# Cosine attention and a multiplicative FFN in one kernel: another order of copies and products in the start-up, and the features of the second batch one by one among the weight-product blocks

## The chip, the cores and the metric

The kernel runs on one core of one Trainium2 chip. The time is the device time of one execution in microseconds (us). Five engines work side by side, each through its own instructions in order: TensorE (PE in the profile, with PEld for its weight loads), VectorE (DVE), ScalarE (ACT), GpSimd (POOL) and SyncE (SP). Here POOL issues all loads, and SP all stores.

## The reference

For 8 batches, 8 heads, 576 positions and 64 elements per head, q and k are made into features of 128 elements (the positive part times a cosine, and times a sine, of the position). Attention without softmax follows, and its output x, 4608 tokens of 512, goes through a feed-forward network (FFN) that multiplies two products:

```python
q_p = phi(q, cos_w, sin_w)
k_p = phi(k, cos_w, sin_w)
kv = np.einsum('bhsf,bhsd->bhfd', k_p, v)
z = np.sum(k_p, axis=2)
num = np.einsum('bhsf,bhfd->bhsd', q_p, kv)
den = np.einsum('bhsf,bhf->bhs', q_p, z)[..., None] + 1e-06
...
a = x @ w1
b = x @ w2
h = a * b @ w3
return (h @ w_out).astype(np.float32)
```

The kernel forms w34 = w3 @ w_out once, so that the last two products become one.

## The kernel before, in words

All of it is one stream that is written out by hand: the order of the calls in the code is the order on every engine.

A batch has 576 positions: five chunks, four of 128 rows and one of 64. `prep_k`, `prep_q` and `prep_v` make one chunk's features: the cosine half of `kp` or `qp` on DVE (L182), the sine half on ACT (L184), and a copy of v into `va` (L196; on DVE for batches 0 and 1, on POOL later). `kv_chunk` multiplies a chunk's `kp` and `va` into a PSUM tile `pnum` over all heads (L212); after the last chunk one half of it is copied to `kvs` by ACT (L217) and the other by DVE (L218). `q_tr` turns a chunk of `qp` over (8 transposes on PE into a PSUM tile `pst`, L226), and DVE copies the result to `qpT` (L227). `num` multiplies `qpT` by `kvs` (L237), and DVE divides by the denominator in three instructions (L241, L242, L244), which gives `xblk`. `x_tr` turns `xblk` over (L263), and ACT copies it into `xT` (L264).

The FFN goes over nine tiles t of 512 tokens. `ffn_groups(t)` is a generator of 24 steps: for each of eight blocks jc of the inner dimension, four products with `w1b` (L303, evicted by ACT as `asb`, L306) and four with `w2b` (L310, multiplied by DVE into `abT`, L312), then for four output blocks eight products with `w34b` (L317), evicted by ACT (L322) and stored. At each step the loop at the end of the kernel puts other work, from a list `slots`, behind the products. During tile t the attention of batch t+1 and the features of later batches run in these slots.

The start-up is batch 0 by itself: features of k and q, `q_tr` and `prep_v` in turns, `kv_chunk`, then `num` and `x_tr` in turns. Its chunks 0 to 3 fill tile 0. Chunk 4 goes in slots 1 and 3. 32 products of a tile of zeros at the very start (`idle_mms`, L120) give PE something to do while the first loads come.

In slot 15 of tile 0 stands the forming of w34: for each of eight row blocks jp, `w3_tr` transposes a block of w3 (L154), DVE copies five eighths of it and ACT three eighths (L156, L157), and `w34_mm` does eight products with `woutb` (L164), which ACT copies into `w34b` (L166). Behind block jp = 1 come all ten k features of batch 1, behind 2 all q features, behind 3 all v copies, and behind 4 to 7 the first attention units of batch 1. `pst` has two buffers, `w3T` two, `ffnps` four.

POOL issues the loads in the order k, q, v of batch 0, `w1b` and `w2b` in three pieces each, `woutb`, then the eight blocks `w3b` mixed with k, q and v of batch 1, then batch 2.

Of the kernel before, what the change touches and what calls it, by code (L numbers as in the profile page):

```python
# [16 lines left out]
P = 128  # L17
H, S, D = 8, 576, 64
F = 2 * D
NCH = 5  # L20
# [31 lines left out]
def kernel(  # L52
# [28 lines left out]
    ps_first = first.enter_context(tc.tile_pool(name="ps_first", bufs=2, space=bass.MemoryType.PSUM))  # L81
# [33 lines left out]

    def idle_mms(n):

        w = ps_first.tile([P, 2, 512], FP32, name="pfirst")
        for _ in range(n):
            nc.tensor.matmul(w[:, 0, :], lhsT=zeros[:, 0:128], rhs=zeros[:], start=True, stop=True)  # L120
# [30 lines left out]
    def w3_tr(jp):  # L151
# [4 lines left out]
        nc.vector.tensor_copy(out=w3T[:, 0:5, :], in_=pst[:, 0:5, :])  # L156
        nc.scalar.copy(out=w3T[:, 5:8, :], in_=pst[:, 5:8, :])  # L157
        w3Ts[jp] = w3T

    def w34_mm(jp):  # L160
        acc = ps_ffn.tile([P, 512], FP32, name="ffnps")
        w3T = w3Ts.pop(jp)
        for lc in range(8):
            nc.tensor.matmul(acc[:, :], lhsT=w3T[:, lc, :], rhs=woutb[:, lc, :],  # L164
                             start=(lc == 0), stop=(lc == 7))
        nc.scalar.copy(out=w34b[:, jp, :], in_=acc[:, :])  # L166
# [54 lines left out]
    def q_tr(b, c):  # L221
# [5 lines left out]
        nc.vector.tensor_copy(out=att_of(b)["qpT"][:, :, ds(128 * c, R)], in_=pst[:, :, 0:R])  # L227

    def num(b, c):
        R = ROWS[c]  # L230
        qpT, kvs = att[b]["qpT"], att[b]["kvs"]
        if b == 0 and c < 4:
# [64 lines left out]
    def ffn_groups(t):  # L297
        x = xT[t]
        abT = fsb.tile([P, 8, 512], BF16, name="abT", bufs=2)
        for jc in range(8):  # L300
            aT = ps_ffn.tile([P, 512], FP32, name="ffnps")
            for kc in range(4):
                nc.tensor.matmul(aT[:, :], lhsT=w1b[:, kc, ts(jc, 128)], rhs=x[:, kc, :],  # L303
                                 start=(kc == 0), stop=(kc == 3))
# [4 lines left out]
            for kc in range(4):  # L309
                nc.tensor.matmul(bT[:, :], lhsT=w2b[:, kc, ts(jc, 128)], rhs=x[:, kc, :],  # L310
                                 start=(kc == 0), stop=(kc == 3))
# [16 lines left out]
    def prep_units(b):  # L328
        return [(lambda f=f, c=c: f(b, c)) for f in (prep_k, prep_v, prep_q) for c in range(NCH)]
# [23 lines left out]
    for t in range(NT):  # L353
        slots = [[] for _ in range(24)]
        if t == 0:
            slots[1].append(lambda: num(0, 4))
            slots[3].append(lambda: x_tr(0, 4))
            slots[14].append(lambda: w3_tr(0))
            w = slots[15]
# [62 lines left out]
```

## Time and profile before

| | |
|---|---|
| median of 3 runs | 287.17 us |
| these runs | 286.15, 287.17, 352.44 us |
| the profiled execution | 288.88 us |
| its span, first to last instruction | 287.1 us |
| PE busy | 270.8 us, 94% |
| PE's weight loads | 143.8 us, 50% |
| DVE / ACT / POOL busy | 149.8 / 144.0 / 61.0 us |
| granted TensorE clock, mean | 0.982 |

Of the profiled time 1.8 us lie outside the span. PE is busy 94% of the span, so what can be gained stands where PE is idle, or busy at a lower clock: the places must be looked up by stage. Busy time is not work: a product at half the clock is busy twice as long.

### The profile page before, as it was taken

Reading aid. Unit: us, or ns where it says so; the run is one execution under the profiler, and the core shown is the slowest. Engines: PE = TensorE matmul, PEld = TensorE weight load, DVE = VectorE, ACT = ScalarE, POOL = GpSimd, SP = SyncE. Lnnn points to the kernel's source line nnn. Section 1 sums busy time; section 2 is a strip of 40 time slices with the busy share of each in tenths; the row PEclk is TensorE's granted clock in tenths of the full one; section 3 lists DMA queues with packets and bytes.
Section 4 is the critical chain, followed back from the end, with each engine's and each line's share of the span. In section 5 each row is a group of like instructions: output and inputs, shape, how many; then the busy total and the mean of one; then the engine's idle time right before and its main releaser. Section 6 shows DMA issues by size and latency. Waiting matters only on the chain.

```text
span 287.1 us, 5398 instructions
## 1 busy us (share of the span) xinstructions
PE 270.8 (94%) x2144; PEld 143.8 (50%) x2144; DVE 149.8 (52%) x356; ACT 144.0 (50%) x254; POOL 61.0 (21%) x101
## 2 busy tenths in 40 slices
PE   8668999789999999999999999999999999999993
PEld 3353455455555555555555555555555555444441
DVE  4672457126468747773686467447634752321420
ACT  2813337722697386268537644863572235324331
POOL 8631443710035323305110810000000000000000
PEclk9995999889999999999999999999999999999999
DMA  7999999991459597937493910330041005006005
GB/s 97 196 202 208 204 203 202 199 198 33 106 85 188 71 211 119 135 66 116 79 163 70 130 35 3 75 73 2 0 110 39 0 12 133 8 0 146 0 22 128
DMA packets 36490, 29.20 MB, mean 102 GB/s; under 512 B 2160, under 2 KB 30832, under 8 KB 36464
## 3 DMA queue, kind: packets, MB, share of 16 engines
q0 software_dynamic: 30704, 19.40, 48.1%
q1 hardware_dynamic: 5760, 9.44, 13.4%
q8 instruction: 17, 0.28, 0.4%
q14 instruction: 9, 0.07, 0.1%
HBM read 38.80 MB, written 9.44 MB: 168 GB/s over the span
## 4 chain that ended last, share of the span: by engine, by line
PE 73%; DMA 15%; ACT 5%; POOL 3%; DVE 2%; issue 1%; POOLq 0%; ACTq 0%
PE ffnps L317 22%; PE ffnps L310 18%; PE ffnps L303 17%; DMA ks<-in_k_dram 6%; PE pst L226 5%; DMA w2b<-in_moe_w_dram 4%; PE pnum L237 3%; DMA w3b<-in_moe_w_dram 3%; PE pnum L212 3%; PE ffnps L164 3%; PE pst L263 3%; ACT kp L184 2%; DMA vs<-in_v_dram 2%; ACT qp L184 1%; DVE kp L182 1%
## 5 line engine op out<-in xcount | busy, mean ns | idle before, releaser
L312 DVE TENSOR_TENSOR abT<-asb,ffnps 128x512 bf16<-128x512 bf16 x72 | 49.3, 685 | 77.6 <-PE ffnps L310 70.9
L306 ACT CAST asb<-ffnps 128x512 bf16<-128x512 f32 x72 | 42.1, 585 | 76.9 <-PE ffnps L303 74.8
L303 PE MATMUL ffnps<-xT,w1b 128*128 128x512 bf16 x288 | 74.7, 382 | 0.7 <-ACT xT L264 0.7
L310 PE MATMUL ffnps<-xT,w2b 128*128 128x512 bf16 x288 | 74.9, 383 | 0.0
L317 PE MATMUL ffnps<-w34b,abT 128*128 128x512 bf16 x288 | 70.9, 379 | 0.0
L303 PEld LDWEIGHTS <-w1b 128*128 128x128 bf16 x288 | 26.2, 98 | 26.1 <-issue 1.4
L310 PEld LDWEIGHTS <-w2b 128*128 128x128 bf16 x288 | 25.2, 98 | 24.4 <-issue 1.1
L317 PEld LDWEIGHTS <-abT 128*128 128x128 bf16 x288 | 25.6, 98 | 23.5
L322 ACT COPY osb<-ffnps 128x512 f32<-128x512 f32 x36 | 21.1, 586 | 24.9 <-PE ffnps L317 21.1
L227 DVE COPY qpT<-pst 128x1024 bf16<-128x1024 bf16 (+1 forms) x40 | 25.2, 630 | 10.8 <-PE pst L226 10.8
L184 ACT ACTIVATE kp<-ks,sinv 128x512 bf16<-128x512 bf16 (+1 forms) x40 | 26.9, 717 | 5.0 <-DMA ks<-in_k_dram 5.0
L264 ACT COPY xT<-pst 128x512 bf16<-128x512 bf16 (+1 forms) x40 | 21.7, 543 | 14.9 <-PE pst L263 14.1
L184 ACT ACTIVATE qp<-qs,sinv 128x512 bf16<-128x512 bf16 (+1 forms) x40 | 27.2, 719 | 0.5 <-DMA qs<-in_q_dram 0.5
L226 PE MATMUL pst<-identb,qp 128*128 128x128 bf16 (+1 forms) x320 | 22.7, 213 | 3.9 <-ACT qp L184 2.4
L226 PEld LDWEIGHTS <-qp 128*128 128x128 bf16 (+1 forms) x320 | 19.0, 97 | 14.0 <-ACT qp L184 3.7
L244 DVE TENSOR_TENSOR xblk<-pnum,den 128x512 bf16<-128x512 f32 (+1 forms) x36 | 24.8, 689 | 1.2
L237 PEld LDWEIGHTS <-qpT 128*128 128x128 bf16 (+1 forms) x320 | 15.0, 102 | 12.6 <-issue 4.1
L164 PE MATMUL ffnps<-woutb,w3T 128*128 128x512 bf16 x64 | 16.8, 405 | 2.0 <-ACT w3T L157 2.0
L212 PEld LDWEIGHTS <-kp 128*128 128x128 bf16 (+1 forms) x320 | 14.0, 97 | 9.0 <-issue 3.1
L196 POOL COPY va<-vs 128x512 bf16<-128x512 bf16 (+1 forms) x30 | 17.4, 636 | 2.4 <-PE pnum L212 2.4
L182 DVE TENSOR_SCALAR kp<-ks,cosv 128x512 bf16<-128x512 bf16 (+1 forms) x40 | 17.1, 459 | 0.6 <-DMA ks<-in_k_dram 0.6
L263 PEld LDWEIGHTS <-xblk 128*128 128x128 bf16 (+1 forms) x160 | 11.0, 99 | 12.1 <-DVE xblk L244 3.1
(51 smaller groups left out, 176.2 us busy)
## 6 DMA issues: line engine op xcount, KB each, us to landing
out_dram<-osb SPq DMA_DIRECT2D x72, 128.0 KB, 2.4
ks<-in_k_dram POOLq DMA_DIRECT2D x8, 320.0 KB, 5.1
qs<-in_q_dram POOLq DMA_DIRECT2D x8, 320.0 KB, 6.4
vs<-in_v_dram POOLq DMA_DIRECT2D x8, 320.0 KB, 7.2
ks<-in_k_dram POOLq DMA_DIRECT2D x8, 256.0 KB, 6.1
qs<-in_q_dram POOLq DMA_DIRECT2D x8, 256.0 KB, 7.0
vs<-in_v_dram POOLq DMA_DIRECT2D x8, 256.0 KB, 8.4
w3b<-in_moe_w_dram POOLq DMA_DIRECT2D x8, 256.0 KB, 15.6
```

What stands on the lines that cost most here:

```text
L164: nc.tensor.matmul(acc[:, :], lhsT=w3T[:, lc, :], rhs=woutb[:, lc, :], start=(lc == 0), stop=(lc == 7))
L184: nc.scalar.activation(out=dst[:R, c, :, D:F], in_=src[:R, :, c, :], func=ACTF.Relu, scale=sinv[:R, c:c + 1], bias=0.0)
L212: nc.tensor.matmul(kvt[:, h // 4, ds((h % 4) * 65, 65)], lhsT=kp[:R, c, h, :], rhs=va[:R, c, h, 0:D + 1], start=(c == 0 and h % 4 == 0), s ...
L226: nc.tensor.transpose(pst[:, h, 0:R], qp[:R, c, h, :], identb[:R, :R])
L227: nc.vector.tensor_copy(out=att_of(b)["qpT"][:, :, ds(128 * c, R)], in_=pst[:, :, 0:R])
L237: nc.tensor.matmul(nt[:R, h // 4, ds((h % 4) * 65, 65)], lhsT=qpT[:, h, ds(128 * c, R)], rhs=kvs[:, h, :], start=True, stop=True)
L244: nc.vector.tensor_tensor(out=xblk[:R], in0=n4[:, :, :, 0:D], in1=den[:R].unsqueeze(3).to_broadcast([R, 2, 4, D]), op=ALU.mult)
L303: nc.tensor.matmul(aT[:, :], lhsT=w1b[:, kc, ts(jc, 128)], rhs=x[:, kc, :], start=(kc == 0), stop=(kc == 3))
L306: nc.scalar.copy(out=asb[:], in_=aT[:, :])
L310: nc.tensor.matmul(bT[:, :], lhsT=w2b[:, kc, ts(jc, 128)], rhs=x[:, kc, :], start=(kc == 0), stop=(kc == 3))
L312: nc.vector.tensor_mul(out=abT[:, jc, :], in0=asb[:], in1=bT[:, :])
L317: nc.tensor.matmul(ops[:, :], lhsT=abT[:, jc, ts(ms, 128)], rhs=w34b[:, jc, :], start=(jc == 0), stop=(jc == 7))
```

## The change

Three pieces, all in tile 0 or ahead of it; from tile 1 on the instructions and their order are the same on every engine.

1. The order in the start-up. `q_tr` of chunks 0 and 1 goes first, then the five v copies in a row, then `q_tr` of chunks 2 and 3, whose copies to `qpT` are now ACT's, then `kv_chunk`, and `q_tr` of chunk 4 only behind it. `num` of chunks 1 and 3 uses the buffer `pnum`, chunks 0 and 2 share one `pfirst`. Eight products of zeros into a tile that nobody reads (`unread`) stand at five places among this work.
2. The first FFN products of tile 0. For jc = 0 and 1, all four products (w1 and w2) are done on tokens 0 to 255 first, and then on tokens 256 to 511; `x_tr` of chunk 3 stands between. Chunk 4's `num` and `x_tr` move from slots 1 and 3 to 4 and 6.
3. The w34 blocks. DVE alone copies `w3T`. Each block's eight products are two parts of four, which gives 16 gaps. The 15 feature units of batch 1 are spread one or two at a time over gaps 4 to 12, in the order k, q, v, and the first ten attention units over gaps 10 to 15.

```diff
-    ps_first = first.enter_context(tc.tile_pool(name="ps_first", bufs=2, space=bass.MemoryType.PSUM))
+    ps_first = first.enter_context(tc.tile_pool(name="ps_first", bufs=1, space=bass.MemoryType.PSUM))
...
+    unread = ps_first.tile([P, 512], FP32, name="unread")
...
-        nc.vector.tensor_copy(out=w3T[:, 0:5, :], in_=pst[:, 0:5, :])
-        nc.scalar.copy(out=w3T[:, 5:8, :], in_=pst[:, 5:8, :])
+        nc.vector.tensor_copy(out=w3T[:], in_=pst[:])
...
+        if t == 0:
+            acc = [ps_ffn.tile([P, 512], FP32, name="ffnps") for _ in range(4)]
+            for half in range(2):
+                for i in range(4):
+                    products(acc[i], (w1b, w2b)[i % 2], i // 2, ts(half, 256))
+                    if i % 2 == 1:
+                        if half:
+                            to_abT(i // 2, acc[i - 1], acc[i])
+                        yield
...
-    for c in range(NCH):
-        q_tr(0, c)
-        prep_v(0, c)
-    for c in range(NCH):
-        kv_chunk(0, c)
-    for c in range(4):
-        num(0, c)
-        if c >= 1:
-            x_tr(0, c - 1)
-    x_tr(0, 3)
+    q_tr(0, 0)
+    q_tr(0, 1)
+    idle_mms(1)
+    for c in range(NCH):
+        prep_v(0, c)
+    copy2 = q_tr(0, 2, evac=False)
+    copy2[1]()
+    copy3 = q_tr(0, 3, evac=False)
+    for c in range(NCH):
+        kv_chunk(0, c)
+    copy3[1]()
+    q_tr(0, 4)
+    idle_mms(2)
+    num(0, 0)
+    num(0, 1)
+    idle_mms(2)
+    num(0, 2)
+    x_tr(0, 0)
+    idle_mms(1)
+    num(0, 3)
+    x_tr(0, 1)
+    idle_mms(2)
+    x_tr(0, 2)
...
-            slots[1].append(lambda: num(0, 4))
-            slots[3].append(lambda: x_tr(0, 4))
+            slots[0].append(lambda: x_tr(0, 3))
+            slots[4].append(lambda: num(0, 4))
+            slots[6].append(lambda: x_tr(0, 4))
...
-            extra = {
-                1: [(lambda c=c: prep_k(1, c)) for c in range(NCH)],
-                2: [(lambda c=c: prep_q(1, c)) for c in range(NCH)],
-                3: [(lambda c=c: prep_v(1, c)) for c in range(NCH)],
-                4: att1[0:3],
...
+            between = [[] for _ in range(16)]
+            spread(prep_units(1, (prep_k, prep_q, prep_v)), 4, 12, between)
+            spread(att1[:10], 10, 15, between)
             for jp in range(8):
-                if jp < 7:
-                    w.append(lambda jp=jp: w3_tr(jp + 1))
-                w.append(lambda jp=jp: w34_mm(jp))
-                w += extra.get(jp, [])
+                for part in range(2):
+                    if part == 0 and jp < 7:
+                        slots[15].append(lambda jp=jp: w3_tr(jp + 1))
+                    slots[15].append(lambda jp=jp, part=part: w34_mm(jp, part))
+                    slots[15] += between[2 * jp + part]
```

Here `copy2[1]` and `copy3[1]` are the copies of `q_tr` on ACT; `products` is the loop over the four products, on the columns that it is given.

On DVE, in the start-up from the last q feature to the copy of `kvs`, there stood:

```order
L182 TENSOR_SCALAR qp<-qs,cosv 64x8x64
L227 COPY qpT<-pst 128x8x128
L196 COPY va_162<-vs 128x8x64
L227 COPY qpT<-pst 128x8x128
L196 COPY va_162<-vs 128x8x64
L227 COPY qpT<-pst 128x8x128
L196 COPY va_162<-vs 128x8x64
L227 COPY qpT<-pst 128x8x128
L196 COPY va_162<-vs 128x8x64
L227 COPY qpT<-pst 128x8x64
L196 COPY va_162<-vs 64x8x64
L218 CAST kvs<-pnum 128x260
```

and now stands:

```order
L186 TENSOR_SCALAR qp<-qs,cosv 64x8x64
L232 COPY qpT<-pst 128x8x128 x2
L200 COPY va_162<-vs 128x8x64 x4
L200 COPY va_162<-vs 64x8x64
L222 CAST kvs<-pnum 128x260
L232 COPY qpT<-pst 128x8x64
```

Of the five copies to `qpT`, those of chunks 2 and 3 have left DVE (ACT does them), that of chunk 4 stands behind `kvs`, and nothing stands between the five v copies.

On ACT, in the middle of the w34 blocks, there stood (w3T is its three eighths of the transposed block, w34b the eviction, kp and qp the features of batch 1):

```order
L166 CAST w34b<-ffnps 128x512
L184 ACTIVATE kp<-ks,sinv 128x8x64 x4
L184 ACTIVATE kp<-ks,sinv 64x8x64
L157 COPY w3T<-pst 128x384
L166 CAST w34b<-ffnps 128x512
L184 ACTIVATE qp<-qs,sinv 128x8x64 x4
L184 ACTIVATE qp<-qs,sinv 64x8x64
L157 COPY w3T<-pst 128x384
L166 CAST w34b<-ffnps 128x512
```

and now stands:

```order
L170 CAST w34b<-ffnps 128x512 x2
L188 ACTIVATE kp<-ks,sinv 128x8x64 x2
L170 CAST w34b<-ffnps 128x512
L188 ACTIVATE kp<-ks,sinv 128x8x64 x2
L188 ACTIVATE kp<-ks,sinv 64x8x64
L170 CAST w34b<-ffnps 128x512
L188 ACTIVATE qp<-qs,sinv 128x8x64 x4
L170 CAST w34b<-ffnps 128x512
L188 ACTIVATE qp<-qs,sinv 64x8x64
```

No copy of `w3T`, for which PE's next products would wait, stands behind features on ACT any more. On DVE the same blocks now read:

```order
L157 COPY w3T<-pst 128x1024 x3
L186 TENSOR_SCALAR kp<-ks,cosv 128x8x64 x4
L157 COPY w3T<-pst 128x1024
L186 TENSOR_SCALAR kp<-ks,cosv 64x8x64
L186 TENSOR_SCALAR qp<-qs,cosv 128x8x64 x2
L157 COPY w3T<-pst 128x1024
L186 TENSOR_SCALAR qp<-qs,cosv 128x8x64 x2
L186 TENSOR_SCALAR qp<-qs,cosv 64x8x64
L157 COPY w3T<-pst 128x1024
L200 COPY va_164<-vs 128x8x64 x4
```

The copies of v (`va_164`) are still DVE's, and the copy of `w3T` of block jp = 6 now stands directly ahead of them.

More of the change, by code (lines that the diff above doesn't have):

```diff
@@ L155, in w3_tr, with w34_mm @@
         w3T = wst.tile([P, 8, 128], BF16, name="w3T")
[L156 to L157 removed]
+        nc.vector.tensor_copy(out=w3T[:], in_=pst[:])
         w3Ts[jp] = w3T
[L160 to L163, printed above, removed]
+    w34_acc = {}
+    def w34_mm(jp, part):
+        if part == 0:
+            w34_acc[jp] = ps_ffn.tile([P, 512], FP32, name="ffnps")
+        acc, w3T = w34_acc[jp], w3Ts[jp]
+        for lc in range(4 * part, 4 * part + 4):
             nc.tensor.matmul(acc[:, :], lhsT=w3T[:, lc, :], rhs=woutb[:, lc, :],
                              start=(lc == 0), stop=(lc == 7))
[L166 removed]
+        if part == 1:
+            nc.scalar.copy(out=w34b[:, jp, :], in_=acc[:, :])
     feat = {}
```

41 lines of the change are left out of this document (22 added, 19 removed).

## Prediction

> **What bounds the kernel now.** I read the busy time by stage first, because a share over the whole span hides where PE waits. The columns are the stretch, its length, busy time and instructions of PE, PEld, DVE, ACT and POOL, the granted clock, the DMA share and GB/s.
>
> ```profile
> core 0: us, PE busy (x) PEld busy (x) DVE busy (x) ACT busy (x) POOL busy (x), PEclk, DMA share, GB/s
> 11.70:18.20 6.50, 4.52 (x84) 3.96 (x85) 4.79 (x14) 2.80 (x5) 2.79 (x6) 1.00 1.44 197
> 18.20:21.60 3.40, 1.88 (x39) 1.53 (x37) 2.81 (x10) 0.69 (x2) 1.16 (x2) 0.97 1.25 207
> 21.60:24.40 2.80, 1.47 (x13) 0.88 (x11) 1.41 (x4) 1.66 (x3) 0.69 (x1) 0.50 1.24 207
> 24.40:28.40 4.00, 3.98 (x16) 1.46 (x15) 0.30 (x1) 0.59 (x1) 0.56 (x1) 0.52 1.25 209
> 28.40:41.30 12.90, 12.90 (x72) 6.01 (x70) 5.95 (x11) 4.63 (x9) 5.53 (x9) 1.00 1.25 205
> 41.30:52.30 11.00, 10.54 (x78) 5.66 (x76) 6.94 (x21) 8.34 (x16) 5.08 (x9) 1.00 1.32 201
> 52.30:55.80 3.50, 1.99 (x32) 1.53 (x33) 0.28 (x1) 2.90 (x6) 2.22 (x4) 0.96 1.41 198
> 55.80:59.20 3.40, 3.40 (x14) 1.53 (x12) 0.63 (x2) 0.48 (x1) 2.60 (x5) 0.54 1.39 199
> 59.20:66.80 7.60, 6.54 (x83) 4.33 (x81) 2.64 (x7) 2.46 (x5) 0.00 (x0) 1.00 1.12 157
> 66.80:76.90 10.10, 9.96 (x98) 5.77 (x95) 6.83 (x18) 3.85 (x9) 0.00 (x0) 1.00 0.31 72
> 76.90:287.10 210.20, 205.01 (x1611) 107.69 (x1608) 111.58 (x247) 110.16 (x194) 30.91 (x49) 1.00 0.44 77
> ```
>
> From 66.8 us on PE is full (9.96 of 10.10, then 205 of 210, its tail included), and the instructions there are the same before and after. So whatever lead PE has where the first output product starts (66.8) stays to the end, and the whole question is the first 66.8 us. There PE has two thin stretches, 18.2 to 24.4 and 52.3 to 55.8, and behind each the clock is at one half: from 21.6 to 28.4 and from 55.8 to 59.2. The second half of the first loss is paid while PE is fully busy (24.4 to 28.4). Loads run at some 200 GB/s until about 65 us whatever PE does.
>
> **The start-up.** The timeline gives each step's length and, in brackets, the idle time ahead of it with its releaser.
>
> ```profile
> 12.43 0.67 DVE L227 COPY qpT<-pst 128x1024 bf16<-128x1024 bf16 x1
> ...
> 13.91 0.29 DVE L196 COPY va<-vs 128x512 bf16<-128x512 bf16 x1 [0.80 <-DMA vs<-in_v_dram]
> ...
> 14.85 0.61 PE L226 MATMUL pst<-identb,qp 128*128 128x128 bf16 x8 [1.09 <-DVE qpT L227]
> ...
> 15.97 1.61 PE L212 MATMUL pnum<-va,kp 128*128 128x65 bf16 x40
> ...
> 17.63 0.38 ACT L217 CAST kvs<-pnum 128x260 bf16<-128x260 f32 x1 [3.50 <-PE pnum L212]
> ...
> 18.84 0.17 DVE L241 TENSOR_SCALAR den<-pfirst 128x8 f32<-128x8 f32 x1 [0.38 <-PE pfirst L237]
> ...
> 22.39 0.69 DVE L244 TENSOR_TENSOR xblk<-pfirst,den 128x512 bf16<-128x512 f32 x1
> ...
> 23.78 0.59 ACT L264 COPY xT<-pst 128x512 bf16<-128x512 bf16 x1 [0.45 <-PE pst L263]
> 24.42 1.87 PE L303 MATMUL ffnps<-xT,w1b 128*128 128x512 bf16 x4 [0.67 <-ACT xT L264]
> ...
> 30.46 1.04 PE L303 MATMUL ffnps<-xT,w1b 128*128 128x512 bf16 x4
> 30.57 0.37 ACT L264 COPY xT<-pst 128x256 bf16<-128x256 bf16 x1 [0.50 <-PE pst L263]
> ...
> 32.20 1.03 PE L303 MATMUL ffnps<-xT,w1b 128*128 128x512 bf16 x4
> ...
> 33.93 1.03 PE L303 MATMUL ffnps<-xT,w1b 128*128 128x512 bf16 x4
> ```
>
> DVE bounds it: v copies and `qpT` copies in turns keep the fourth chunk's transposes waiting 1.09 us, and `kv_chunk` starts at 15.97. In the changed order the second `qpT` copy ends about 13.8 (two of 0.67 from 12.43), the v copies start at 13.91 as now, when v is there, and take at most 5 x 0.29 = 1.4 us. The transposes of chunk 3 go from 13.85 to 14.45, and the 40 products behind them start there instead of at 15.97: **1.5 us**. They end at 16.1; chunk 4's transposes and two zero products fit while ACT and DVE make `kvs`. The first denominator comes at 17.4 for 18.84, and four groups of three instructions from 18.84 to 23.08 are 1.06 each, so the four `xblk` end at 18.5, 19.5, 20.6 and 21.6.
>
> ACT's copies of 128x1024 do not occur before. 0.37 us for 256 columns and 0.59 for 512 give 1.03 for 1024; bounds are 0.59 and 1.18 (twice the 512). I take 1.03: chunk 2's runs from 14.1 to 15.2, ahead of `kvs` at 16.1; chunk 3's from 16.5 to 17.5, needed at 19.5. Either bound is hidden; without that 0.9 us of cover, an excess would hold up `kvs` and all behind it one for one.
>
> Now the half tiles. The first FFN products need only chunks 0 and 1 in `xT`: `num` of chunk 3, whose buffer is free when the second `xblk` is done, and `x_tr` of chunk 1 run behind 19.55 (some 0.42 and 0.45), PE is through at 20.45, ACT (0.59) at 21.05, so PE starts at 21.1 instead of 24.42. Two pairs of half products take 0.87 each at full clock (eight whole ones take 32.20 to 33.93 = 1.73), with `x_tr` of chunk 3 between them; its `xT` copy ends at 23.05, just when PE wants the second half, and that ends at 24.85. Splitting 16 products into 32 adds issue cost: I take 0, between 0 and 0.3 us (eight transposes of 128 columns with their loads come in 0.61 us, so a product of 256 should not be bound by its load). In the kernel before, the start of jc = 2 is 30.46, with `num` and `x_tr` of chunk 4 done: twelve short products, some 0.04 us each as the 40 in 1.61, 0.45 together at full clock. The same state is reached at 24.85 + 0.45 = 25.3: a **lead of 5.1 us**. About 2 of it is the clock: 24.42 to 28.4 at half speed.
>
> This takes for granted that the clock stays up. The rows on it:
>
> ```profile
> 2.03 0.15 PEld L120 LDWEIGHTS <-zeros 128*128 128x128 bf16 x1 [0.28 <-issue]
> ...
> 4.46 4.85 PEld L120 LDWEIGHTS <-zeros 128*128 128x128 bf16 x23 [0.15 <-issue]
> ```
>
> Zero products raise the clock: at the start they come every 0.43 us, after 4.46 us every 0.21 (4.85 over 23). PE was 55% busy in the 3.4 us ahead of the first fall and 57% ahead of the second; at 70% (11.7 to 18.2) it did not fall. With the zero products and the denser order my schedule leaves PE idle about 0.65 us between 17.85 and 18.5 and little after that, some 85% busy between 18.2 and 21.6. So I take no fall. The eight zero products cost 8 x 0.216 = 1.7 us of PE, all in waits for DVE by this schedule; if the waits were gone, they would cost up to that.
>
> The Trainium skill, "TensorE: Matmul & The Clock Gate", section "What's actually happening", has the gate fall after an idle window of about 3.4 us, and its windows free-running. By the first half of that, nothing here should have fallen and filling short gaps could save nothing; the trace shows falls behind stretches that were half busy, so I go by the trace. The second half means that where a window cuts can differ between executions; it is why a fall remains a rival.
>
> **The w34 blocks**, from 41.28 on:
>
> ```profile
> 41.28 0.61 PE L154 MATMUL pst<-identb,w3b 128*128 128x128 bf16 x8
> ...
> 43.45 0.61 PE L154 MATMUL pst<-identb,w3b 128*128 128x128 bf16 x8
> ...
> 49.90 0.82 PE L164 MATMUL ffnps<-woutb,w3T 128*128 128x512 bf16 x3 [0.41 <-ACT w3T L157]
> 50.22 3.17 ACT L184 ACTIVATE qp<-qs,sinv 128x512 bf16<-128x512 bf16 x5
> ...
> 53.81 0.82 PE L164 MATMUL ffnps<-woutb,w3T 128*128 128x512 bf16 x3 [1.57 <-ACT w3T L157]
> ...
> 56.17 3.26 PE L164 MATMUL ffnps<-woutb,w3T 128*128 128x512 bf16 x8
> ...
> 60.67 1.89 PE L164 MATMUL ffnps<-woutb,w3T 128*128 128x512 bf16 x8
> ...
> 63.98 0.42 PE L237 MATMUL pnum<-kvs,qpT 128*64 128x65 bf16 x8 [1.06 <-DVE kvs L218]
> ```
>
> PE's last three products of a block wait for ACT's part of `w3T`, which stands behind five features on ACT (3.17 us): 0.41 + 1.57 us idle. DVE's single copy of 128x1024 (0.67, the row of 12.43) takes that away; it lies beside PE's products, since DVE is busy 6.94 of these 11.0 us, and if DVE were full its 0.67 would stand ahead of each block. The third wait, 1.06 us for `kvs`, shrinks because four products stand ahead of `num`; 0.25 us is left by my schedule. The half clock costs 3.26 - 1.89 = 1.4 on the eight products and 0.3 on the transposes ahead of them, 1.7. Taken away: 0.41 + 1.57 + 0.8 + 1.7 = 4.5.
>
> What is late next? Blocks come every 2.17 us (41.28 to 43.45), and loads don't move:
>
> ```profile
> w3b<-in_moe_w_dram POOLq DMA_DIRECT2D x1, 256.0 KB, 10.9
> ...
> 36.42 0.56 POOL L108 DMA_DIRECT2D w3b<-in_moe_w_dram  x1 [0.95 <-DMA ks<-in_k_dram]
> ...
> 46.47 0.68 POOL L95 DMA_DIRECT2D qs<-in_q_dram  x1 [0.46 <-DMA vs<-in_v_dram]
> ```
>
> Block 6 of w3, issued at 36.42, lands 10.9 us later, at 47.3. With the lead, its transposes want to start at 36.2 + 5 x 2.17 = 47.05: a new wait of 0.3 (0 to 0.6). v of batch 1 is there at about 46.4, when the POOL row that waits for it goes on; DVE copies it behind block 6's `w3T`, which ends at about 47.3 + 0.61 + 0.67 = 48.6, so the first copy ends at 48.9; PE, through with the transposes and four products of block 5 at about 48.6, waits some 0.35 for it (0 to 0.6). Behind both waits PE holds the rest of block 5, and ACT its eviction, which nobody wants before 57. Together 0.65. The ACT features lie under PE: from 41.0 ten features of 0.63 (3.17 over 5) and four evictions of 0.59 end near 49.7, and the transposes of the last q chunk want it at about 50.6. Net 4.5 - 0.65 = **3.8 us**.
>
> **Sum**: 5.1 + 3.8 = 8.9 us, so the first output product starts at 57.9 and the profiled execution becomes 288.88 - 8.9 = 280.0. The profiled execution stands 1.7 above the median of 287.17; against that median the result is 278.3. Loads of batch 2 and 3 end before about 67 us as now, and are used in tile 1, from 68 on; stores start earlier, at 61, beside the last loads. I cost that at nothing (0 to 0.5).
>
> **Rivals.**
>
> *The clock falls all the same* in one of the two places (20%). A window of 3.4 busy us at half costs 1.7; two windows at the start, as now, 3.4: 280.0 to 281.7. For it: my zero products may stand where PE is not idle, and window edges vary. Against: no stretch under 70% is left.
>
> *The loads take the lead back* (13%). Were block 6 or v of batch 1 to land later than now, each us costs one, up to the lead of 5.1: 283.4 at worst, 280 to 281 likely. For it: the margin is gone (47.05 against 47.3). Against: the queue waits for the same landings as before, and none of its early waits is on an engine that is late.
>
> *Slower* (2%): half the clock holds from the first FFN product to the last block because every window has a small wait. That is 36.8 us, 10.8 windows of 1.7 = 18.4 lost against 8.9 won, 296.7. It decides from the sixth window on. Against: 28.4 to 41.3 is all busy now, and the same products stand there.
>
> My forecast has 62%, own range 277.2 to 279.8; the last 3% is a gain above mine. A measurement of this kernel tells changes of about 2%, 5.7 us, from none. All of the forecast's chance, half of the clock's, most of the loads' and the 3% are above that: faster 0.85, same 0.13, slower 0.02. The range runs from 276.5 (none of the 0.9 us of waits that I count, and 0.9 for runs that lie 1.0 apart) to 282.0 (a fall at the start, with 0.3 for the split).
>
> **What would show it.** `kv_chunk` from 14.5 instead of 15.97; FFN products of 256 columns from 21.1; clock 1.00 in every stretch from 4.5 on; jc = 2 at about 24.9; the w34 products without a wait for ACT; first output product near 57.9. I am wrong if the clock shows 0.50 behind 21, if PE waits for w3b or v by more than 1 us, or if DVE's copies of w3T hold it up.

## The result, and the profile after

| | before | after |
|---|---|---|
| median | 287.17 us (286.15 to 288.50, 3 runs) | 279.75 us (279.58 to 279.92, 4 runs) |
| the profiled execution | 288.88 us | 279.75 us |
| its span | 287.1 us | 278.0 us |
| granted TensorE clock, mean | 0.982 | 1.0 |
| PE busy | 270.8 us | 265.8 us |

One run more of the kernel before (288.50 us) was made beside those of the changed kernel; the one of 352.44 was disturbed and is left out, so that the median of the others is 287.17 as before. After over before is 0.9738, interval 0.9688 to 0.9788: **faster by 7.4 us**. The forecast was 278.3, 8.9 less than before, its range 276.5 to 282.0: the direction and the range hold, and the size was put 1.45 us too large. Between the two profiled executions the span is 9.1 us shorter, where the sum said 8.9. Both differences are small; why one is short and the other is not is the more useful part of what follows.

The busy time by stage of the changed kernel, with the columns of the prediction's table (stretch, length, busy time and instructions of PE, PEld, DVE, ACT and POOL, clock, DMA share, GB/s):

```profile
11.70:18.20 6.50, 5.88 (x100) 4.52 (x101) 4.66 (x16) 4.79 (x8) 2.95 (x5) 1.00 1.44 193
18.20:21.60 3.40, 2.64 (x36) 1.88 (x37) 3.19 (x10) 1.56 (x3) 1.23 (x2) 1.00 1.26 206
21.60:24.40 2.80, 2.80 (x30) 2.53 (x28) 0.19 (x2) 1.37 (x3) 0.69 (x1) 1.00 1.25 208
24.40:28.40 4.00, 3.95 (x30) 2.00 (x30) 2.99 (x6) 1.44 (x3) 0.56 (x1) 1.00 1.24 208
28.40:41.30 12.90, 12.85 (x84) 6.80 (x84) 5.42 (x8) 3.79 (x8) 5.11 (x8) 1.00 1.25 204
41.30:52.30 11.00, 10.37 (x100) 5.97 (x100) 6.99 (x20) 8.57 (x15) 4.75 (x7) 1.00 1.34 200
52.30:57.90 5.60, 5.49 (x63) 3.40 (x64) 3.40 (x9) 1.26 (x3) 3.91 (x7) 1.00 1.40 198
57.90:68.00 10.10, 9.91 (x92) 5.77 (x93) 6.37 (x17) 4.29 (x9) 1.62 (x3) 1.00 1.30 223
68.00:278.00 210.00, 202.86 (x1577) 107.65 (x1606) 111.47 (x247) 109.86 (x194) 30.82 (x49) 1.00 0.44 77
```

The reader is to see two things. The clock column is 1.00 in every row, where before it was 0.50 to 0.54 in three. And the last two rows are those of before, moved: 10.1 and 210 us for 10.1 and 210.2, so whatever was won ahead of the first output product is won for good, as the prediction's reading had it.

The timeline gives that product and the steps ahead of it (start, length, engine, line, operation; in brackets the idle time ahead and its releaser):

```profile
14.21 0.99 ACT L233 COPY qpT<-pst 128x1024 bf16<-128x1024 bf16 x1
14.38 1.10 DVE L200 COPY va<-vs 128x512 bf16<-128x512 bf16 x5 [0.50 <-DMA vs<-in_v_dram]
...
14.73 1.54 PE L216 MATMUL pnum<-va,kp 128*128 128x65 bf16 x40 [0.19 <-DVE va L200]
...
17.52 0.17 DVE L250 TENSOR_SCALAR den<-pfirst 128x8 f32<-128x8 f32 x1
...
21.14 0.60 PE L312 MATMUL ffnps<-xT,w1b 128*128 128x256 bf16 x4
...
24.86 1.03 PE L312 MATMUL ffnps<-xT,w1b 128*128 128x512 bf16 x3
...
36.47 0.61 PE L155 MATMUL pst<-identb,w3b 128*128 128x128 bf16 x8
...
47.73 0.45 PEld L155 LDWEIGHTS <-w3b 128*128 128x128 bf16 x8 [0.73 <-DMA w3b<-in_moe_w_dram]
47.74 0.62 PE L155 MATMUL pst<-identb,w3b 128*128 128x128 bf16 x8 [0.24 <-DMA w3b<-in_moe_w_dram]
...
49.34 0.67 PE L216 MATMUL pnum<-va,kp 128*128 128x65 bf16 x16 [0.34 <-DVE va L200]
...
57.40 0.42 PE L246 MATMUL pnum<-kvs,qpT 128*128 128x65 bf16 x8
57.87 0.81 PE L342 MATMUL ffnps<-w34b,abT 128*128 128x512 bf16 x3
```

The row of 36.47 stood at 41.28 (L154 there): 4.8 us of lead from the start-up. The row of 57.87 lists three products of four: the record of the first is missing. In every profile that lists all four, the first output product starts 0.26 us behind the row of `num` ahead of it, which is here the one of 57.40; so it started at 57.66. It stood at 66.77: 9.1 us, as much as the spans differ, so the blocks added 4.3. PE's longest waits from 11 to 60 us (what waited, for whom, us in total, times, longest) no longer name `w3T` or `kvs`:

```profile
PE pst L230 <- ACT qp L188: 1.7, 1, 1.7
PE pfirst L246 <- DVE xblk L253: 0.5, 1, 0.5
PE pnum L216 <- DVE va L200: 0.5, 2, 0.3
PE pnum L246 <- DVE den L250: 0.3, 1, 0.3
PE pst L155 <- DMA w3b<-in_moe_w_dram: 0.2, 1, 0.2
```

The first row, 1.7 us for a q feature, is a wait ahead of 12.8 us in the start-up, where the kernel before has it too. What is new are the short waits for `va` and for the load of block 6 of w3, the two that the prediction had named.

### The profile page after: what moved, and what is told of

The parts are those of the page before. It is cut to its first block, busy times and chain, and to the rows that moved or that the text cites. A ratio compares the mean times of both kernels' runs of the same rounds, so it can differ in the third digit from the quotient of the medians.

```text
span 278.0 us, 5404 instructions
## 1 busy us (share of the span) xinstructions
PE 265.8 (96%) x2129; PEld 144.1 (52%) x2168; DVE 150.1 (54%) x354; ACT 142.2 (51%) x248; POOL 60.9 (22%) x101
## 4 chain that ended last, share of the span: by engine, by line
PE 74%; DMA 16%; POOL 3%; issue 3%; DVE 2%; ACT 1%; POOLq 0%; ACTq 0%
PE ffnps L312 36%; PE ffnps L342 22%; DMA ks<-in_k_dram 6%; PE pst L230 5%; DMA w3b<-in_moe_w_dram 4%; DMA w2b<-in_moe_w_dram 4%; PE pnum L246 4%; PE pnum L216 3%; PE pst L272 3%; DMA vs<-in_v_dram 2%; PE ffnps L167 2%; ACT kp L188 1%; DVE kp L186 1%; POOL ks L93 1%; POOL w1b L135 1%
## 5 line engine op out<-in xcount | busy, mean ns | idle before, releaser
L337 DVE TENSOR_TENSOR abT<-asb,ffnps 128x512 bf16<-128x512 bf16 x70 | 48.0, 685 | 70.8 <-PE ffnps L312 62.0
L333 ACT CAST asb<-ffnps 128x512 bf16<-128x512 f32 x70 | 40.8, 585 | 73.0 <-PE ffnps L312 73.0
L312 PE MATMUL ffnps<-xT,w1b 128*128 128x512 bf16 (+1 forms) x287 | 73.4, 373 | 0.6
L312 PE MATMUL ffnps<-xT,w2b 128*128 128x512 bf16 (+1 forms) x279 | 72.0, 373 | 0.8 <-issue 0.3
L342 PE MATMUL ffnps<-w34b,abT 128*128 128x512 bf16 x279 | 69.3, 379 | 0.6 <-issue 0.2
L312 PEld LDWEIGHTS <-w1b 128*128 128x128 bf16 x296 | 26.9, 98 | 24.6
L347 ACT COPY osb<-ffnps 128x512 f32<-128x512 f32 x36 | 21.1, 585 | 25.0 <-PE ffnps L342 21.1
L253 DVE TENSOR_TENSOR xblk<-pnum,den 128x512 bf16<-128x512 f32 (+1 forms) x38 | 26.2, 690 | 1.3
L232 DVE COPY qpT<-pst 128x1024 bf16<-128x1024 bf16 (+1 forms) x38 | 23.8, 627 | 5.5 <-PE pst L230 5.5
L230 PEld LDWEIGHTS <-qp 128*128 128x128 bf16 (+1 forms) x320 | 18.9, 97 | 12.8 <-ACT qp L188 3.3
L246 PE MATMUL pnum<-kvs,qpT 128*128 128x65 bf16 (+1 forms) x304 | 16.2, 194 | 0.6 <-DVE den L250 0.3
L216 PE MATMUL pnum<-va,kp 128*128 128x65 bf16 (+1 forms) x320 | 15.9, 193 | 0.5 <-DVE va L200 0.5
```

The costliest lines, as they stand in the source:

```text
L216: nc.tensor.matmul(kvt[:, h // 4, ds((h % 4) * 65, 65)], lhsT=kp[:R, c, h, :], rhs=va[:R, c, h, 0:D + 1], start=(c == 0 and h % 4 == 0), s ...
L230: nc.tensor.transpose(pst[:, h, 0:R], qp[:R, c, h, :], identb[:R, :R])
L232: on_vector = lambda: nc.vector.tensor_copy(out=dst, in_=src)
L246: nc.tensor.matmul(nt[:R, h // 4, ds((h % 4) * 65, 65)], lhsT=qpT[:, h, ds(128 * c, R)], rhs=kvs[:, h, :], start=True, stop=True)
L253: nc.vector.tensor_tensor(out=xblk[:R], in0=n4[:, :, :, 0:D], in1=den[:R].unsqueeze(3).to_broadcast([R, 2, 4, D]), op=ALU.mult)
L312: nc.tensor.matmul(out_ps[:, tok], lhsT=w[:, kc, ts(jc, 128)], rhs=x[:, kc, tok], start=(kc == 0), stop=(kc == 3))
```

## The experiments

Twelve kernels were run in three groups, each group on one chip and beside runs of the kernel before. "Changed" is the kernel after the change.

### The eight zero products taken out

```diff
     q_tr(0, 1)
-    idle_mms(1)
...
-    idle_mms(2)
     num(0, 0)
     num(0, 1)
-    idle_mms(2)
...
-    idle_mms(1)
...
-    idle_mms(2)
```

> The changed kernel without the eight zero products in the gaps of the start-up (the 32 at the very start stay). Theory: PE's share of busy time sets the clock. The 18.2 to 21.6 stretch, 78% busy with them, holds three of them (0.65 us) and goes to about 59%, near the 55% and 57% ahead of which the clock fell before. So the clock falls to one half behind 21 for one or two windows of 3.4 us: 281.4 to 283.1 us against 279.75. Rival: only a window without any work lets the clock fall; then the clock stays at 1.00 and the time at 279.7.

Measured: 280.52 us (280.12 to 281.22), 0.9764 of before [0.9743, 0.9785], with mean clocks of 0.994, 0.994, 0.990 and 0.985. Its busy time by windows of 3.4 us:

```profile
15.90:19.30 3.40, 1.55 (x31) 1.21 (x30) 2.93 (x10) 1.60 (x3) 1.11 (x3) 0.99 1.38 202
19.30:22.70 3.40, 3.25 (x25) 2.41 (x26) 1.79 (x5) 1.24 (x3) 0.99 (x2) 0.51 1.25 206
22.70:26.10 3.40, 3.40 (x32) 2.81 (x31) 0.91 (x2) 1.76 (x3) 0.92 (x2) 1.00 1.24 206
```

Without the zero products PE is busy 1.55 of 3.40 us, and the clock is at half in the next window, though no gap comes near 3.4 us. So a window without any work is not needed, which rules the rival out; that PE's share of busy time alone decides is not shown by this, and the last section says what speaks against it. The price is not as argued. From the first k-v product to the first w3 transposes behind the start-up (block 1) it takes 22.93 us (14.18 to 37.11) and with the zero products 21.74 (14.73 to 36.47): the fall costs 1.2 us and not 1.7, presumably since some of the half clock lies on time in which PE would have waited. At block 1 this kernel is 0.64 us behind the changed one, and by the first output product 0.33 is left (57.99 for 57.66). Where the rest went is asked further below.

### Each half of the change alone

`w34` blocks as before in the changed kernel:

```diff
-        nc.vector.tensor_copy(out=w3T[:], in_=pst[:])
+        nc.vector.tensor_copy(out=w3T[:, 0:5, :], in_=pst[:, 0:5, :])
+        nc.scalar.copy(out=w3T[:, 5:8, :], in_=pst[:, 5:8, :])
...
-            spread(prep_units(1, (prep_k, prep_q, prep_v)), 4, 12, between)
-            spread(att1[:10], 10, 15, between)
+            extra = {
+                1: [(lambda c=c: prep_k(1, c)) for c in range(NCH)],
+                2: [(lambda c=c: prep_q(1, c)) for c in range(NCH)],
+                3: [(lambda c=c: prep_v(1, c)) for c in range(NCH)],
...
```

> The changed kernel with the w34 blocks as before (features in fives, w3T copied by DVE and ACT). Theory: the start-up's lead of 5.0 us stays, and PE waits for ACT's part of w3T again, 1.05 and 2.05 us, since ACT is behind by as much; the clock falls once behind them (1.7 us) and the wait for kvs is 1.06 again. Together some 4.9 us over 279.75: 284.6. Rival: the loads of batch 1 bind these blocks once they run 5 us earlier, and take the lead back: then nearer 287.

And the other way round, the new blocks in the kernel before:

> The kernel before with the new w34 blocks alone. Theory: from the first w3 transposes to the first output product they take 4.1 us less in the changed kernel, of which a wait of 0.3 for block 6 of w3 is given back, and that wait does not come 5 us later: 4.4 us less than before, so 284.5 for an execution like the profiled one of before (288.88) and 282.8 against its median. The clock falls at the start as before, and not in the blocks. Rival: the blocks' gain needs the higher clock of the start-up; then under 3 us.

Measured, against 287.39 us (286.94 to 287.97, 8 runs) of the kernel before on this chip:

| | us | less than before | mean clock |
|---|---|---|---|
| start-up alone | 282.16 (281.69 to 282.43), 0.9821 [0.9803, 0.9840] | 5.2 | 0.997 to 1.0 |
| blocks alone | 284.10 (283.67 to 286.41), 0.9899 [0.9866, 0.9933] | 3.3 | 0.984 to 0.986, once 0.974 |

The two halves add to 8.5 us; the whole change brought 7.4, and 8.4 in the second group below. The start-up brings the 5.1 that was worked out for it, and its run is 2.4 us faster than the 284.6 that I expected: PE's waits for `w3T` are 2.0 us and not 3.1, and the clock does not fall. The blocks bring 3.3, and not the 3.8 of the sum or the 4.4 that I expected of this run. Of the two times that I gave, 284.5 from the profiled execution of before and 282.8 from its median, 284.10 is near the first. PE's waits in the first of the two show the waits of before, unchanged (2.0 on `w3T`, 1.1 on `kvs`):

```profile
PE ffnps L165 <- ACT w3T L158: 2.0, 2, 1.6
PE pnum L243 <- DVE kvs L219: 1.1, 1, 1.1
```

But the clock behind those waits does not fall here:

```profile
46.80:50.20 3.40, 1.91 (x33) 1.45 (x34) 1.86 (x7) 2.90 (x6) 2.06 (x3) 1.00 1.33 198
50.20:53.60 3.40, 3.40 (x47) 2.43 (x45) 1.08 (x3) 1.07 (x2) 1.37 (x2) 1.00 1.40 198
```

PE is busy 1.91 of 3.40 us, no more than the 1.99 of 3.50 ahead of the fall in the profile of before, and the next window has the full clock. So the 1.7 us of half clock in the blocks is not a fixed part of their old order. The same shows in the kernel before itself. Of its 26 timed runs in the three groups, 17 have a mean clock of 0.984 to 0.987 and a median of 287.32 us, and 9 have 0.969 to 0.982 and a median of 288.71. The profiled execution of before, with 0.982 and 288.88, is of the second kind. One window of 3.4 us at half is 1.7 of 287 us, 0.006 of mean clock: by that, the larger group holds the two windows of the start-up (0.988) and no more. The profile of the blocks alone, which has a mean of 0.985, shows what such a mean holds:

```profile
21.44:24.85 3.41, 1.95 (x15) 1.08 (x12) 1.45 (x4) 1.69 (x3) 0.69 (x1) 0.50 1.24 207
24.85:28.26 3.41, 3.41 (x16) 1.22 (x13) 0.28 (x1) 0.59 (x1) 0.56 (x1) 0.50 1.25 208
28.26:280.85 252.59, 248.63 (x1972) 131.91 (x1969) 136.66 (x305) 129.54 (x228) 46.35 (x73) 1.00 0.57 96
280.85:282.32 1.47, 0.00 (x0) 0.00 (x0) 0.00 (x0) 0.00 (x0) 0.00 (x0) 0.50 0.03 8
```

There are the two windows of the start-up, and 1.5 us behind PE's last product, which cost nothing. I have windows of the kernel before from one execution only, so that the further falls of the nine lie in the blocks is concluded from the clock and not seen.

### Splitting the start-up

The first FFN products on the whole tile again, with `x_tr` of chunk 3 ahead of them:

```diff
-            for half in range(2):
-                for i in range(4):
-                    products(acc[i], (w1b, w2b)[i % 2], i // 2, ts(half, 256))
...
+            for i in range(4):
+                products(acc[i], (w1b, w2b)[i % 2], i // 2, slice(0, 512))
...
+    x_tr(0, 3)
...
-            slots[0].append(lambda: x_tr(0, 3))
```

> The changed kernel with its first FFN products on the whole tile (x_tr of chunk 3 ahead of them, all else as changed). Theory: they start when the copy of chunk 3 is done, about 22.9 us, and jc = 2 starts at about 26.3 instead of 24.75: 1.6 us lost, of which 0.3 comes back where block 6 of w3 is waited for: 281.0. Rival: PE's idle time of about 1.3 us ahead of 22.9 lets the clock fall besides: 282.7 or more. Second rival: the loads hide the delay, 279.9.

Measured: 280.38 us (280.19 to 280.63), 0.9757 [0.9741, 0.9773], clock 1.0; 0.6 above the changed kernel's 279.75, or 0.96 above the 279.42 of its repetition below. From the first k-v product to block 1 of w3 it takes 23.21 us (14.04 to 37.25) for 21.74, 1.5 more. So again less arrives than the start-up loses.

The second group began with the changed kernel once more, in more rounds, as the base for the rest:

> The changed kernel itself again, beside the next three. Theory: the profiled execution of before holds two falls of the clock, and its granted mean is 0.982; eight timed executions of before had 0.985 to 0.987, which leaves room for the fall at the start alone. So the 1.7 us of the second fall are no gain against an ordinary execution, and this one lies 7.4 to 8.0 us under before: ratio 0.972 to 0.974. Rival: the gain of the two profiles, 9.1 us, holds in general: 0.968.

Measured: 279.42 us (279.40 to 280.25, 6 runs), 0.9713 [0.9683, 0.9742], with 287.80 for before: 8.4 us less, somewhat more than expected. Against the seven runs of before there whose mean clock is 0.984 to 0.987 (median 287.31) it is 7.9 us less. Its timeline holds a surprise:

```profile
13.72 1.54 PE L216 MATMUL pnum<-va,kp 128*128 128x65 bf16 x40
...
47.40 0.62 PE L155 MATMUL pst<-identb,w3b 128*128 128x128 bf16 x8 [0.91 <-DMA w3b<-in_moe_w_dram]
```

In this execution v landed sooner, and the k-v products started at 13.72 instead of 14.73, 1.0 us earlier. The transposes of block 6 of w3 start at 47.40 instead of 47.74, and the wait ahead of them has grown from 0.24 to 0.91 us. The first output product comes at 57.32 for 57.66: of 1.0 us of lead, 0.3 arrives.

The v copies in turns with the q copies, and all of them DVE's, as before:

```diff
+    prep_v(0, 0)
     q_tr(0, 1)
+    prep_v(0, 1)
     idle_mms(1)
-    for c in range(NCH):
-        prep_v(0, c)
-    copy2 = q_tr(0, 2, evac=False)
-    copy2[1]()
-    copy3 = q_tr(0, 3, evac=False)
+    q_tr(0, 2)
+    prep_v(0, 2)
+    q_tr(0, 3)
+    prep_v(0, 3)
+    q_tr(0, 4)
+    prep_v(0, 4)
     for c in range(NCH):
         kv_chunk(0, c)
-    copy3[1]()
-    q_tr(0, 4)
```

> The changed kernel with the v copies in turns with the q copies again, all on DVE, and all five q transposes ahead of the k-v products. Theory: DVE bounds the start-up again, the k-v products start some 1.2 us later than 14.7, the four xblk about 1.3 later, and some 0.5 of that comes back at the wait for block 6 of w3: 0.8 us more than the changed kernel. Rival: with PE idle longer ahead of the products the clock falls as well: 1.5 to 2.5 more.

Measured: 280.98 us (280.42 to 281.85), 0.9762 [0.9723, 0.9801]: 1.6 above the changed kernel of the same group, where I expected half of that. Two of its four runs have a mean clock of 0.992 and stand at 281.51 and 281.85; the two others stand at 280.42 and 280.44, 1.0 above. The place is where it was expected:

```profile
15.83 1.61 PE L216 MATMUL pnum<-va,kp 128*128 128x65 bf16 x40
```

The products start 2.1 us later than in its sister, as they did before the change. In these two runs, then, the order of the copies is worth 1.0 us of the 2.1; that the other two had a fall of the clock is read from their mean alone.

Twice as many zero products, sixteen:

```diff
-    idle_mms(1)
+    idle_mms(2)
...
-    idle_mms(2)
+    idle_mms(4)
...
```

> The changed kernel with sixteen zero products in the gaps instead of eight (1.7 us more of PE). Theory: the gaps left are 0.2, 0.5 and 0.25 us, so that about half of the added products is hidden, and the copy of chunk 1 to xT covers part of the last two; 0.3 to 0.6 us more than the changed kernel. Rival: PE is the bound of the start-up by now, and all 1.7 us show.

Measured: 279.57 us (279.32 to 279.75), 0.9709 [0.9667, 0.9750]; 0.15 above the changed kernel, within its scatter. Eight further products, 1.7 us of PE work, lengthen the way to block 1 of w3 by 0.6 us (14.43 to 36.76, 22.33), and of these nothing shows in the time.

### Where a lead of up to a microsecond vanishes

Three kernels lose 0.6 to 1.5 us on the way to block 1 of w3, one execution of the changed kernel gains 1.0, and less than that reaches the end. The starts of PE's rows, in us, one profile each (the last five kernels are shown below; the wait is PE's own, in brackets in its row). Where the record of the first output product is missing, as in four of these profiles, its start is taken 0.26 us behind that of `num`:

| kernel | first k-v product | block 1 of w3 | block 6 of w3 | wait there | first output product |
|---|---|---|---|---|---|
| changed | 14.73 | 36.47 | 47.74 | 0.24 | 57.66 |
| changed, repeated | 13.72 | 35.46 | 47.40 | 0.91 | 57.32 |
| no zero products | 14.18 | 37.11 | 47.98 | none | 57.99 |
| whole tile | 14.04 | 37.25 | 48.35 | none (its weight loads 0.56) | 58.27 |
| copies in turns | 15.83 | 37.58 | 48.44 | none | 58.35 |
| zero products twice | 14.43 | 36.76 | 47.62 | none | 57.53 |
| v copies ahead | 14.00 | 35.74 | 47.15 | 0.39 | 56.79 |
| v copies and load ahead | 14.35 | 36.09 | 46.95 | none | 56.59 |
| the same, whole tile | 13.91 | 37.13 | 48.00 | none | 57.63 |
| the same, no zero products | 14.88 | 36.63 | 47.50 | none | 57.22 |
| the same, `w3T` copy split | 13.68 | 35.42 | 46.29 | none | 56.72 |

The first column follows the landing of v by 0.44 us: it differs by 1.2 us between executions, 13.68 to 14.88 (only the copies in turns are late by their order). The second follows the first at 21.74 us in every kernel that leaves the start-up as changed. From block 1 to block 6 it is 10.87 us where nothing is waited for, five blocks of 2.17; in the changed kernel it is 11.27, in its repetition 11.94, and 11.10 on the whole tile, whose weight loads waited. So block 6 of w3 is wanted at the time at which it lands, and that lies between 47.1 and 48.3 us in the profiles with this order of loads. Who comes earlier waits for it, and a start-up that is up to 0.4 us longer than that of the changed kernel loses nothing.

The next kernel moves that load ahead of v of batch 1, and, since v then comes later and the earlier block would run into the wait for it, puts all five v copies in one gap, ahead of block 6's copy on DVE:

```diff
-    load(1, "v")
     load_w3(6)
+    load(1, "v")
...
-            spread(prep_units(1, (prep_k, prep_q, prep_v)), 4, 12, between)
+            spread(prep_units(1, (prep_k, prep_q)), 4, 9, between)
+            between[9] += prep_units(1, (prep_v,))
```

> The changed kernel with block 6 of w3 loaded ahead of batch 1's v, and the five v copies of batch 1 all in the gap ahead of block 6's transposes. Theory: of PE's waits in the w34 blocks those for block 6 (some 0.5 to 0.7 us) and for the first v copies (0.5) go, and no other comes, since block 6's own copy is wanted only three blocks of PE work later: 0.8 to 1.1 us less than the changed kernel. Rival: v now lands 1.3 us later and holds up DVE, the wait moves to the k-v products: 0 to 0.4 less.

Measured: **278.70 us** (278.55 to 278.96, 6 runs), 0.9682 [0.9654, 0.9710] of before; 0.7 below the changed kernel of its group. No wait of PE over 0.2 us is left from 40 to 60 us. Block 6's transposes and the first output products (three of four on record; the first at 56.59):

```profile
46.95 0.61 PE L155 MATMUL pst<-identb,w3b 128*128 128x128 bf16 x8
...
56.80 0.81 PE L342 MATMUL ffnps<-w34b,abT 128*128 128x512 bf16 x3
```

No kernel with the old loads had block 6 at 46.95. This version beats both kernels, and in it a start that is earlier or later can be seen in the time, so the remaining questions were put to it. The third group ran on another chip; the kernel before has 288.28 there. First its two halves apart, the v copies ahead and the loads in the old order:

```diff
-    load_w3(6)
     load(1, "v")
+    load_w3(6)
```

> The changed kernel (279.4) with the v copies of batch 1 ahead of block 6's transposes alone, loads in their old order. Theory: the wait for the first v copies (0.5 us) goes and the wait for block 6 (0.6 to 0.9) stays: 0.3 to 0.5 us less. Rival: both waits have one cause, the late loads, and the time stays at 279.4.

Measured: 279.16 us (278.87 to 279.94), 0.9693 [0.9653, 0.9734]. PE waits for block 6 and no longer for `va`:

```profile
47.15 0.62 PE L155 MATMUL pst<-identb,w3b 128*128 128x128 bf16 x8 [0.39 <-DMA w3b<-in_moe_w_dram]
```

By that some 0.3 of the 0.7 us is the v copies' and the rest the load's; differences of this size between two chips lie within the scatter of the runs. The profiles agree on the part of the v copies: the first output product comes 9.64 us behind block 6 in both kernels that have them ahead, and 9.92 in the two executions of the changed kernel.

The whole tile again, now without the load in the way:

> The same kernel (278.7) with the first FFN products on the whole tile. Theory: with the load wait gone, the delay of jc = 2 shows in full; it was 0.9 us in the first run of this edit and 1.6 by the prediction's steps: 0.9 to 1.6 us over 278.7. Rival: 0.6 as in the first run.

Measured: 280.12 us (279.85 to 280.33), 0.9725 [0.9679, 0.9770], 1.4 above 278.70. The first products:

```profile
22.07 1.02 PE L312 MATMUL ffnps<-xT,w1b 128*128 128x512 bf16 x4 [0.67 <-ACT xT L273]
...
25.52 1.03 PE L312 MATMUL ffnps<-xT,w1b 128*128 128x512 bf16 x4
```

PE waits 0.64 us ahead of chunk 3's transposes and 0.67 behind them, for ACT's copies to `xT`. From the first k-v product to jc = 2 it takes 11.6 us (13.91 to 25.52), and with half tiles 10.1 (14.35 to 24.47). So the half tile is worth 1.4 to 1.5 us in the start-up and in the time; with the old loads the wait for block 6 gave part of it back, and 0.6 to 1.0 was left.

The zero products out of this version:

> The kernel with the other load order and the v copies ahead (278.7 us), without the eight zero products in the gaps. In the first run without them the clock fell for one window of 3.4 us, and the wait for block 6 of w3, which takes up to 1 us off any delay of the start-up, hid part of the price. Theory: here that wait is gone and the whole price shows, half a window or more less the 0.3 us that the zero products themselves cost: 0.8 to 1.5 us over 278.7. Rival: the price is the 0.4 to 0.8 us of the first run, load wait or not.

Measured: 279.11 us, 0.9703 [0.9644, 0.9762], but the runs are 278.39, 278.90, 279.32 and 281.64, with clocks of 1.0, 0.994, 1.0 and 0.986. Its profile is of an execution without a fall:

```profile
18.20:21.60 3.40, 1.96 (x31) 1.53 (x32) 3.19 (x10) 1.41 (x3) 0.72 (x2) 1.00 1.26 206
```

PE is busy 1.96 of 3.40 us here, as it was ahead of falls in other kernels, and nothing falls; the last section shows that the windows by which the clock goes cut elsewhere in this execution. So the expectation of a fall in every run was wrong. Where the clock stays up, the zero products change nothing on the way to block 1: 21.75 us without them (14.88 to 36.63) and 21.74 with them. They hardly move the median (0.4 us), and seem to buy evenness: the four runs without them lie 3.3 us apart, most of it by a single one (281.64), and the six with them 0.4.

### Who took away the waits for `w3T`

The copy of `w3T` split between DVE and ACT again, all else as in the best version:

```diff
-        nc.vector.tensor_copy(out=w3T[:], in_=pst[:])
+        nc.vector.tensor_copy(out=w3T[:, 0:5, :], in_=pst[:, 0:5, :])
+        nc.scalar.copy(out=w3T[:, 5:8, :], in_=pst[:, 5:8, :])
```

> The same kernel (278.7) with w3T copied by DVE and ACT in shares of five and three eighths again, features one by one. The prediction put the end of PE's two waits in the w34 blocks (2.0 us) down to DVE's single copy. Theory A, that step: the split brings most of them back, 1 to 2 us. Theory B: the spreading of the features did it; ACT's part now stands behind an eviction and two or three features (1.9 us at most), and PE wants it 2.6 us after the end of the block before, so that 0 to 0.3 us come back.

Measured: 279.08 us (278.83 to 279.67), 0.9689 [0.9650, 0.9729], 0.4 above 278.70. PE does not wait for `w3T`. What it waits for is the last q feature of ACT, once:

```profile
49.07 0.74 ACT L189 ACTIVATE qp<-qs,sinv 64x512 bf16<-64x512 bf16 x1
49.70 0.47 ACT L158 COPY w3T<-pst 128x384 bf16<-128x384 bf16 x1
49.86 0.40 PE L231 MATMUL pst<-identb,qp 64*128 64x64 bf16 x8 [0.50 <-ACT qp L189]
```

With three features between two of ACT's copies there in the place of five, the copy is in time whoever makes it. Beside the spread features, the single copy on DVE only relieves ACT of 0.47 us a block, which is worth the 0.5 us of this wait. (From block 6 to the first output product this profile takes 0.8 us more than that of the best version; the other 0.2 to 0.3 are a wait for v of batch 1, which had not landed when this execution, 0.7 us ahead, wanted it.) The reverse, a single copy on DVE with the features still in fives, was not run, so whether it would have been enough by itself is not shown.

## Why the prediction was right or wrong, by its steps

- **The bound** (PE full from the first output product on): right; 210.0 us are left behind it, 210.2 before.
- **The start-up lead of 5.1 us**: right, 4.8 in the profiles (36.47 for 41.28), where v landed 0.5 us later than in the profile of before, and 5.2 in the run with the start-up alone. The first half products came at 21.14 for 21.1, jc = 2 at 24.86 for 24.85. The k-v products came later than said (14.73 for 14.45), since v landed later: DVE's first v copy started at 14.38 and not at 13.91. I had carried the landing over as a fixed time; by the table above it has a scatter of 1.2 us.
- **ACT's copies of 128x1024**, estimated at 1.03 us: 0.99, hidden.
- **No fall of the clock, the zero products hidden**: right for this kernel, whose profiles show no fall, and the way to block 1 is the same with and without zero products at full clock. The reason, a busy share under which the clock falls, does not hold as it was put: the stretch from 11.7 to 18.2 us, read as 70% busy, runs over a window (11.16 to 14.57) in which PE was 54% busy, and the clock stayed up. The price that I set on a fall, 1.7 us for each window, was too large: a fall cost 1.2 on the way to block 1 of w3, and without the zero products the median loses 0.4 to 1.1. Single executions can lose more (281.64 where others have 278.39, both without the zero products).
- **New waits in the blocks, 0.3 and 0.35**: right in place and size, 0.24 and 0.34 for PE; block 6 came 0.4 us later than its blocks' pace.
- **"DVE's single copy of 128x1024 takes that away"**, of the 2.0 us of waits for ACT's `w3T`: the gain is there, the reason is not the one needed. Splitting the copy again, beside the spread features, left PE without such a wait; the spreading of the features takes it away without the single copy. Whether the single copy would do so without the spreading is open.
- **1.7 us of half clock in the blocks, and 1.7 from the profiled execution to the median**: here the size failed, and both are one mistake. The profiled execution of before held a fall of the clock in the blocks that most executions of that kernel do not have; that is why it stood above the median. The sum took the fall away as a gain, 4.5 instead of 2.8 us gross in the blocks, and the last step then took the same 1.4 to 1.7 us off again, as a distance between profile and median that the changed kernel would keep; so the 278.3 of the forecast is too low by about that much. It did not keep it: its median and its profiled execution are both 279.75, against the 280.0 of the sum. That the sum comes so near is partly luck: the start-up brought 0.3 less than it said and the blocks 0.5 more (4.3 for 3.8). The runs of the two halves bear it out: 3.3 us for the blocks where the start-up keeps its falls, and old blocks at the full clock where it does not.
- **The rivals**: the clock fell in no profile of the changed kernel. The loads did take some lead back, in the way that the rival said and within the 0.3 that the sum had for it; of a further 1.0 us of lead in the repeated run 0.7 was lost to it.

## What to carry to other kernels

Before a gain from the clock is counted against a median, compare the clock and the time of the profiled execution with those of the other runs: where it is slow by the price of one fall, that fall belongs to this execution, and it may not be taken off twice. A lead in the start-up lives only as long as the next load lands ahead of it; look for the first load that is wanted at the time at which it lands, and move its issue together with the work. When one edit changes who copies and also when the work around it comes, undo them one at a time before either gets the credit.

## What the runs showed of the hardware

**The clock falls behind half-busy windows, and not behind all of them.** In the profile of before the half clock runs from 21.4 to 28.2 us and from 55.5 to 58.9: lengths and distances are multiples of 3.41 us. Full clock begins there at 4.33 us, under the zero products, five such steps ahead of 21.4. Counted in these steps from the beginning of the full clock, the windows of each profile can be placed (an estimate). Two of before, one of the old blocks behind the new start-up, and one of the best version without zero products:

```profile
17.98:21.39 3.41, 1.82 (x35) 1.47 (x35) 2.77 (x10) 0.61 (x2) 1.24 (x2) 1.00 1.25 207
52.12:55.53 3.41, 1.84 (x30) 1.26 (x30) 0.01 (x1) 3.08 (x7) 2.13 (x4) 1.00 1.40 197
46.73:50.15 3.42, 1.86 (x32) 1.40 (x33) 1.81 (x7) 2.97 (x6) 2.06 (x3) 1.00 1.32 198
18.48:21.90 3.42, 2.26 (x34) 1.79 (x35) 3.21 (x10) 1.71 (x3) 1.02 (x2) 1.00 1.25 207
```

The first two, 53% and 54% busy, were followed by half clock, and so were 47% (zero products out) and 55% (blocks alone). The third, 54%, was not, nor were 51% (changed, 8.64 to 12.06 us), 54% (before, 11.16 to 14.57) and 56% (whole tile with the loads ahead). No window of over 56% was followed by a fall, and none ahead of a fall in the start-up or the blocks held a gap of PE near 3.4 us. The fourth row fits that: the window there begins at 18.48 and not at 18.20, and its busy share is 66% and not 58%, so the clock stayed up without zero products. The Trainium skill, "TensorE: Matmul & The Clock Gate", section "What's actually happening", has the fall come after an idle window of about 3.4 us: these windows were half busy, so the trace differs there. The same section has the windows free-running, so that where they cut varies from run to run: that agrees with the beginning of the full clock, at 4.3 to 7.2 us in the fourteen profiles, and with 17 and 9 of 26 runs of one kernel, 1.4 us apart. PE's busy share does not decide between 47% and 56%; what does stays open.

**The landing of a queued load can pin everything behind it.** Between 34.15 and 35.16 us, the starts of block 0 in the repeated and the first run of the changed kernel, there is 1.0 us; between the starts of block 6 behind its load, 0.34. Issued ahead of v, the load was no longer waited for.
